# A decode attention kernel rewritten as one critical section with recorded semaphores and a TensorE loop over the head groups

## The chip, the cores and the metric

The kernel runs on one core of a Trainium2 chip (trn2). The metric is the device time of one execution in microseconds (us). The kernel before takes 667.5 us (median of nine runs of a batch, 667.4 to 667.8), and executions agree within 0.1%. A difference of half a microsecond is therefore readable, though it is under 0.1% of the time.

"TensorE" is PE in the profile, "VectorE" is DVE, "ScalarE" is ACT, and SP is the engine that issues the large loads.

## The reference, cut to what matters

One token for each of four sequences goes through an attention block over a cached K and V and then through a small gated MLP. Nearly all bytes are the two caches.

```python
# A_x (4, 1, 512); k_cache, v_cache (4, 32, 4096, 128), bfloat16: 134 MB each
q = (x @ wq).reshape(B, Sq, H, Dh).transpose(0, 2, 1, 3)
scores = einsum('bhqd,bhkd->bhqk', q, k_cache) * Dh ** -0.5
p = softmax(scores)
o = einsum('bhqk,bhkd->bhqd', p, v_cache)
attn = o.transpose(0, 2, 1, 3).reshape(B, Sq, H * Dh) @ wo
...                      # x + ga * attn, layernorm, gated MLP with w_in and w_out
```

## The kernel before

Work is cut into 32 "quads": four heads (one head group g of eight) of one sequence b. A quad's K is one 4 MiB load, its V another. Two K buffers and two V buffers alternate. VectorE multiplies K by the query in place, TensorE sums the products by 32 matmuls against an identity, VectorE finishes the sum ("fold"), the softmax follows, and TensorE multiplies the probabilities by V one quad later. The values are divided by the softmax sum and projected two quads later. Every engine's instructions are written out 32 times.

```python
def load(cache, i, tag, parts):
    t = kvp.tile([P, NT * DH], BF16, name=tag, bufs=2)       # 128 x 16384: 4 MiB
    ...
        nc.sync.dma_start(out=t[:, a:b], in_=kv_view(cache, i)[:, a:b])
...
def scores(i, half):
    nc.vector.tensor_tensor(out=kt, in0=kt, in1=q[...], op=ALU.mult)
    ps = psum.tile([P, HT, DC], F32, name="s_ps", bufs=2)
    for cc in range(DH // DC):
        nc.tensor.matmul(ps, lhsT=ident, rhs=kt[:, :, cc * DC:(cc + 1) * DC], ...)
...
for i in range(NQ):                                          # NQ = 32
    if i + 1 < NQ:
        st["k", i + 1] = load_k(i + 1)
    ...
    st["v", i] = load_v(i)
    if i == NQ - 1:
        ...                                                  # wo_l, win, wout: the last weights
    if i > 1:
        diagonal(i - 2)
    ...
    scores(i, 0)
    if i > 1:
        project(i - 2)
    scores(i, 1)
    if i == NQ - 1:
        softmax(i - 1)
    fold(i, 0)
    fold(i, 1)
    if i != NQ - 2:
        softmax(i)
    if i > 0:
        values(i - 1)
    if i > 1:
        apply(i - 2)
```

After the loop come the last projection with `wo_l`, a layer norm, the MLP with `win` and `wout`, and a 4 KB output.

## Time and profile before

| what | before |
|---|---|
| time, median | 667.5 us |
| span of the profiled execution | 665.5 us |
| bytes moved, mean rate | 283.17 MB, 426 GB/s |
| busy share: DMA main queue, PE, DVE | 98.9%, 62%, 61% |
| issue to landing of a K load, of a V load | 26.0 us, 33.7 us |

From the profile's page of the kernel before: busy time by engine; the span in 40 slices, where each digit is a busy share in tenths; and the DMA queues, with packets, megabytes and the share of the time of 16 engines.

```profile
PE 415.7 (62%) x3024; PEld 204.6 (31%) x3024; DVE 402.6 (61%) x475; ACT 41.3 (6%) x115; POOL 4.7 (1%) x21
...
DMA  9999999999999999999999999999999999999995
...
q1 hardware_dynamic: 12640, 282.73, 98.9%
q8 instruction: 23, 0.38, 0.2%
q14 instruction: 6, 0.05, 0.0%
```

DMA stands at 9 tenths until the last slice while no compute engine passes two thirds: the stream of loads is the limit. The page calls two small queues "instruction". Queue 8 moved 23 blocks of 16 KiB. Queue 14 moved six packets of 8 KiB.

The end of the chain of waits of the kernel before, as start, duration and what it is:

```profile
651.74 9.15 DMA wout_437<-in_B_w_out_dram
...
660.93 0.50 PE y_ps L522 x12
...
662.82 0.28 DVE ot L544
```

The last load, `wout`, lands at 660.89, and 12 matmuls and a few short steps follow. The same stretch by windows of one microsecond (window, length, busy share and count for PE, PEld, DVE, ACT and POOL, then PE clock, DMA share, GB/s):

```profile
655.00:656.00 1.00, 0.58 (x2) 0.50 (x2) 0.42 (x3) 0.00 (x0) 0.00 (x0) 0.50 1.01 404
656.00:657.00 1.00, 0.06 (x1) 0.00 (x0) 0.77 (x5) 0.29 (x1) 0.00 (x0) 0.50 0.67 260
657.00:658.00 1.00, 0.19 (x6) 0.22 (x7) 0.35 (x2) 0.95 (x3) 0.00 (x0) 0.50 0.58 235
658.00:659.00 1.00, 1.00 (x35) 1.00 (x33) 0.00 (x0) 0.55 (x1) 0.00 (x0) 0.50 0.57 234
659.00:660.00 1.00, 1.00 (x27) 0.97 (x25) 0.19 (x1) 0.41 (x2) 0.00 (x0) 0.50 0.48 193
660.00:661.00 1.00, 0.90 (x20) 0.76 (x20) 0.73 (x5) 0.99 (x1) 0.00 (x0) 0.50 0.16 61
```

From 656 on the DMA share falls to about a half, not to zero. The 16 DMA engines do not finish together: in the trace's records the last weight load's 16 semaphore increments (one for each engine) lie between 656.07 and 660.89, seven within 1.1 us and nine 3.1 to 4.8 us later.

### The profile page before, as it was taken

The numbers are of one execution on the slowest core, as the hardware profiler recorded it, in microseconds if no ns is written. First come the engines' busy times: TensorE is split into PE (matmuls) and PEld (weight loads), VectorE is DVE, ScalarE is ACT, GpSimd is POOL, SyncE is SP. The second block draws the span as 40 slices with busy tenths as digits, with TensorE's granted clock in tenths as the row PEclk, the third lists the DMA queues.
The fourth block names the chain that finished last, engine by engine and source line by source line (L and its number), as shares of the span: only waits on it lengthen the run. The fifth ranks groups of instructions, "written<-read, shape, count | busy, mean of one in ns | idle before, by whom it ended". The sixth has DMA issues, their size and how long they took to land.

```text
span 665.5 us, 6939 instructions
## 1 busy us (share of the span) xinstructions
PE 415.7 (62%) x3024; PEld 204.6 (31%) x3024; DVE 402.6 (61%) x475; ACT 41.3 (6%) x115; POOL 4.7 (1%) x21
## 2 busy tenths in 40 slices
PE   2557776655677655676555477654657655657775
PEld 2223333222333322233222233232223322223334
DVE  2166776675556576547666456666555666655762
ACT  1200000000000000000000000000000000000002
POOL 2000000000000000000000000000000000000000
PEclk9977777668887667887667788676888766888795
DMA  9999999999999999999999999999999999999995
GB/s 379 439 425 427 437 439 424 429 438 434 427 428 441 428 428 434 435 426 434 433 436 424 436 435 430 423 439 435 428 431 435 433 430 432 437 426 435 428 417 236
DMA packets 12749, 283.17 MB, mean 426 GB/s; under 512 B 1448, under 2 KB 1968, under 8 KB 4016
## 3 DMA queue, kind: packets, MB, share of 16 engines
q1 hardware_dynamic: 12640, 282.73, 98.9%
q8 instruction: 23, 0.38, 0.2%
q14 instruction: 6, 0.05, 0.0%
q0 software_dynamic: 64, 0.00, 0.0%
q10 hardware_dynamic: 16, 0.01, 0.0%
HBM read 282.73 MB, written 0.00 MB: 425 GB/s over the span
## 4 chain that ended last, share of the span: by engine, by line
DMA 62%; PE 24%; DVE 12%; issue 0%; SPq 0%; ACT 0%; DVEq 0%
DMA kt<-in_A_k_cache_dram 58%; PE s_ps L281 24%; DVE kt L276 11%; DMA vt<-in_A_v_cache_dram 3%; DMA wout_437<-in_B_w_out_dram 1%; PE big L341 0%; DVE S L290 0%; ACT E L311 0%; SPq L92 0%; DVE P_1_109 L314 0%; DVE P_0_105 L314 0%; PE y_ps L522 0%; DVE nm L308 0%; DVE mT L300 0%; SPq L78 0%
## 5 line engine op out<-in xcount | busy, mean ns | idle before, releaser
L281 PE MATMUL s_ps<-kt,ident 128*128 128x512 bf16 x1024 | 293.5, 457 | 185.5 <-DVE kt L276 185.5
L276 DVE TENSOR_TENSOR kt<-kt,qbc 128x8192 bf16<-128x8192 bf16 x64 | 282.7, 4420 | 82.9 <-DMA kt<-in_A_k_cache_dram 82.9
L281 PEld LDWEIGHTS <-ident 128*128 128x128 bf16 x1024 | 116.4, 114 | 351.1 <-issue 229.8
L290 DVE TENSOR_REDUCE S<-s_ps 128x64 f32<-128x512 f32 x64 | 44.3, 692 | 125.5 <-PE s_ps L281 125.5
L354 PE MATMUL zo_ps<-sel,osb 128*128 128x4 f32 x248 | 33.2, 257 | 26.6 <-ACT osb L347 26.6
L311 ACT ACTIVATE E<-S,nm 128x128 f32<-128x128 f32 x32 | 12.8, 401 | 563.4 <-DVE nm L308 563.4
L354 PEld LDWEIGHTS zo_ps<-sel,osb 128*128 128x128 f32 x248 | 30.6, 194 | 38.4 <-ACT osb L347 38.4
L341 PE MATMUL big<-vt,P_0_105 128*32 128x512 bf16 x352 | 21.0, 380 | 1.5 <-DMA vt<-in_A_v_cache_dram 1.5
L341 PE MATMUL big<-vt,P_1_109 128*32 128x512 bf16 x320 | 19.1, 380 | 0.0
L341 PE MATMUL big<-vt,P_2_113 128*32 128x512 bf16 x320 | 19.1, 380 | 0.0
L347 ACT COPY osb<-big 128x512 f32<-128x512 f32 x31 | 17.6, 566 | 20.0 <-PE big L341 20.0
L215 PE MATMUL big<-vt,hbc 128*32 128x512 bf16 x128 | 9.6, 471 | 5.2 <-DMA vt<-in_A_wq_dram 5.2
L314 DVE TENSOR_TENSOR P_1_109<-E,mask_99 128x512 bf16<-128x512 f32 x11 | 7.6, 692 | 6.8 <-ACT E L311 6.8
L314 DVE TENSOR_TENSOR P_0_105<-E,mask_99 128x512 bf16<-128x512 f32 x11 | 7.6, 692 | 6.7 <-ACT E L311 6.7
L341 PEld LDWEIGHTS <-P_0_105 128*32 128x32 bf16 x352 | 8.4, 96 | 8.9 <-DMA vt<-in_A_v_cache_dram 1.6
L314 DVE TENSOR_TENSOR P_2_113<-E,mask_99 128x512 bf16<-128x512 f32 x10 | 6.9, 692 | 6.2 <-ACT E L311 6.2
L400 PE MATMUL attn_ps<-oP,wo_g 128*128 128x4 bf16 x112 | 3.8, 164 | 10.6 <-DVE oP L397 10.6
L341 PEld LDWEIGHTS <-P_1_109 128*32 128x32 bf16 x320 | 7.6, 96 | 6.7
L341 PEld LDWEIGHTS <-P_2_113 128*32 128x32 bf16 x320 | 7.6, 96 | 6.7
L375 DVE TENSOR_TENSOR oT<-zo_ps,rz 128x4 bf16<-128x4 f32 x32 | 5.4, 168 | 7.1 <-PE zo_ps L363 6.0
L215 PEld LDWEIGHTS <-hbc 128*32 128x32 bf16 x128 | 4.4, 114 | 10.3 <-issue 8.4
L308 DVE STREAM_TRANSPOSE nm<-hb 128x32 f32<-128x32 f32 x32 | 6.8, 212 | 1.1
(221 smaller groups left out, 131.1 us busy)
## 6 DMA issues: line engine op xcount, KB each, us to landing
kt<-in_A_k_cache_dram SPq DMA_DIRECT2D x31, 4096.0 KB, 26.0
vt<-in_A_v_cache_dram SPq DMA_DIRECT2D x31, 4096.0 KB, 33.7
vt<-in_A_wq_dram SPq DMA_DIRECT2D x1, 4096.0 KB, 20.4
kt<-in_A_k_cache_dram SPq DMA_DIRECT2D x2, 2048.0 KB, 24.8
wo_g<-in_A_wo_dram SPq DMA_DIRECT2D x7, 512.0 KB, 26.5
vt<-in_w_mod_dram SPq DMA_DIRECT2D x1, 3072.0 KB, 9.8
vt<-in_A_v_cache_dram SPq DMA_DIRECT2D x1, 2048.0 KB, 17.8
win_434<-in_B_w_in_dram SPq DMA_DIRECT2D x1, 1344.0 KB
```

Of the source, the lines that this page charges most:

```text
L215: nc.tensor.matmul(qp[hl * R:(hl + 1) * R, 0:n], lhsT=hbc[:, j, b, :], rhs=wv[:, g0:g0 + n, hl, :], start=(j == 0), stop=(j == J - 1), til ...
L276: nc.vector.tensor_tensor(out=kt, in0=kt, in1=q[:, None, :].to_broadcast([P, HT, DH]), op=ALU.mult,)
L281: nc.tensor.matmul(ps, lhsT=ident, rhs=kt[:, :, cc * DC:(cc + 1) * DC], start=(cc == 0), stop=(cc == DH // DC - 1),)
L290: nc.vector.tensor_reduce(out=st["S", i][:, half * HT:(half + 1) * HT], in_=st.pop(("s", i, half)), axis=AX.X, op=ALU.add,)
L308: nc.vector.transpose(out=nm, in_=hb)
L311: nc.scalar.activation(out=E, in_=S, func=AF.Exp, bias=nm[:, 0:1], scale=att_scale, accum_out=rs,)
L314: nc.vector.tensor_tensor(out=P4[:, 0:NT, :], in0=E[:, :, None].to_broadcast([P, NT, NH]), in1=mask4[:, None, :].to_broadcast([P, NT, NH]) ...
L341: nc.tensor.matmul(po[32 * t:32 * t + 32], lhsT=P4[:, n0:n0 + 8, :], rhs=st["v", i][:, n0:n0 + 4, :], start=(u == 0), stop=(u == NU - 1), ...
L347: nc.scalar.copy(out=osb, in_=po)
L354: nc.tensor.matmul(st["o", i], lhsT=osb[:, n, :], rhs=sel[:, NH * n:NH * n + NH], start=(n == 0), stop=(n == 3),)
L375: nc.vector.tensor_tensor(out=oT[:, :, b], in0=st.pop(("o", i)), in1=rz, op=ALU.mult,)
L400: nc.tensor.matmul(attn_ps[:, jo, :], lhsT=(wo_g[:, hl] if g < G - 1 else wo_l[hl // 2][:, hl % 2])[:, jo * P:(jo + 1) * P], rhs=oT[:, hl, :],
```

## The change

The intent is a much smaller program for TensorE. All operations are first recorded, with the semaphore waits worked out from the tiles they touch. One critical section then issues them: four engines in straight code, and TensorE's four-quad body as a hardware loop run eight times. To make all eight turns alike, the pipeline's empty start is filled with zeros, and the softmax of a quad is done one step later. Each buffer's loads have a semaphore lane of their own. The K and V buffers become four named tiles that ask for a start at a multiple of 128 bytes. The core of the diff:

```diff
-    ctx.enter_context(tc.manual_schedule())
+    nc = Recorder(tc.nc, tc)
...
-        return kvp.tile([P, cols], BF16, name="vt", bufs=2)
+    vts = [kvp.tile([P, NT * DH], BF16, name=f"vt{a}", align_bytes=128) for a in range(2)]
+    kts = [kvp.tile([P, NT * DH], BF16, name=f"kt{a}", align_bytes=128) for a in range(2)]
...
+                if e == "tensor" and lo <= k < hi:
...
+                        with engine.Fori(0, periods, 1) as it:
+                            for group, steps in zip(body, plan):
+                                for sm, v, d in steps:
+                                    engine.wait_ge(sm, it * d + v)
+                                issue(group[0])
...
-            if i > 1:
-                diagonal(i - 2)
-            if i == NQ - 1:
-                keep_busy(4)
-            scores(i, 0)
-            if i > 1:
-                project(i - 2)
-            scores(i, 1)
-            if i == NQ - 1:
-                softmax(i - 1)
-            fold(i, 0)
-            fold(i, 1)
-            if i != NQ - 2:
-                softmax(i)
-            if i > 0:
-                values(i - 1)
-            if i > 1:
-                apply(i - 2)
+            diagonal(b2)
+            scores(g, b, 0)
+            project(b2)
+            scores(g, b, 1)
+            softmax(b1)
+            fold(b, 0)
+            fold(b, 1)
+            values(b1)
+            if b2 == B - 1:
+                apply()
...
+        for t in (oTt, osbs[0], Ss[B - 1], wo_g):
+            nc.gpsimd.memset(t, 0.0)
...
+        with tc.tile_critical():
+            nc.emit(G)
```

## The prediction

> **What bounds the kernel now.** The stream from HBM. The page: 283.17 MB at 426 GB/s, the main queue takes 98.9% of 16 engines' span, and in the slices DMA stands at 9 tenths in all but the last. PE is busy 62%, DVE 61%. The chain of waits is 62% DMA; its PE and DVE pieces are links by which buffers come free, not lost time: a K load is issued 26.0 us before it lands and a V load 33.7 us, while 4 MiB at 430 GB/s take 9.8 us (estimate), so 14 to 16 us of transfers stand queued ahead.
>
> Not stream: 0.75 us to the first issue, 4.6 us from the last landing (660.89) to the end. One more loss: in one-microsecond stretches the DMA share falls from 1.01 (655 to 656) to 0.67, 0.58, 0.57, 0.48, 0.16. The engines don't finish together. The 16 semaphore increments of the last weight load lie between 656.07 and 660.89: seven within 1.1 us, nine 3.1 to 4.8 us later; at 31 us, fifteen lay within 0.6 us. The gap grows in steps of about 1.3 us, one engine at a time, as queue 8 (instructions) moves 23 blocks of 16 KiB: PE's 6,048 matmuls and weight loads. So instruction fetch delays nine engines two or three times each.
>
> **What the change does.**
> - TensorE's four-quad body becomes a loop run 8 times: 308 matmuls (about 670 instructions with weight loads, 2.6 blocks, estimate), 780 in all. HBM bytes for K, V and weights stay.
> - [...]5 to 7 blocks are fetched instead of 23: at most one step per engine, the stream ends 2.5 to 3 us earlier. If every turn fetches again, 30 to 38 blocks: +1 to +2.5 us. [...] I give staying 60%.
> - [...]
> - The previous quad's softmax (about 2.6 us by its lines) stands between DVE's products and folds, while PE still sums. Values stay where they were in PE's order; V buffers free no later.
> - Zero work for absent quads and extra POOL memsets (done before 15 us, PE needs them at 31): hidden.
> - A semaphore for each load: last weights issue earlier than 643 to 652. The queue wasn't empty there: no gain.
> - [...]
>
> **Prediction:** 665.7 us; 663.7 to 669.8 should hold it 8 times in 10. Faster by over 2%: 0.01; within 2%: 0.97; slower by over 2%: 0.02.
>
> **Shown right by:** DMA at 9 tenths throughout; K and V landings near 26 and 34 us; instruction-queue packets well under 23 and a steeper fall of the DMA share at the end (resident), or over 30 and a longer tail (fetched again); DVE's and PE's busy times within 3%.
>
> **Wrong if:** back-edge stalls reach 10 us and drain the queue (holes every 80 us), or PE loses weight-load overlap in the loop, or placement of tiles changes the stream's rate.

The sum came to 665.7 us, 1.8 us less than before: 2.5 to 3 us less if the loop's blocks are fetched once for all eight turns ("staying", "resident"), 1 to 2.5 us more if every turn fetches again, and a small addition for the critical section's handshakes.

## The result, and the profile after

The changed kernel takes 668.5 us (median of four runs, 668.40 to 668.67) against 667.5 us (667.41 to 667.67) for the kernel before in the same rounds. The ratio is 1.0015, with a 95% interval of 0.9998 to 1.0032: the same within 2%. A ratio here is the mean time of one kernel's fast runs over that of the other's of the same rounds, so it is not quite the ratio of the medians quoted beside it.

The lines of the page of the kernel after that answer to those of before:

```profile
PE 421.2 (63%) x3105; PEld 205.2 (31%) x3105; DVE 401.8 (60%) x487; ACT 45.6 (7%) x118; POOL 8.4 (1%) x27
...
DMA  9999999999999999999999999999999999999995
...
q1 hardware_dynamic: 12640, 282.73, 98.8%
q8 instruction: 6, 0.10, 0.1%
q14 instruction: 6, 0.05, 0.0%
...
kt<-in_A_k_cache_dram SPq DMA_DIRECT2D x31, 4096.0 KB, 25.7
vt<-in_A_v_cache_dram SPq DMA_DIRECT2D x31, 4096.0 KB, 33.7
```

Queue 8 moves 6 blocks instead of 23: four by 79 us, two after 652 us, none between, while the loop turns. The stream is as full as before, landings take the same time, and PE and DVE are busy within 1.4% of before. The end by windows of the kernel after, with the same columns:

```profile
656.00:657.00 1.00, 0.64 (x2) 0.50 (x2) 0.36 (x3) 0.00 (x0) 0.00 (x0) 0.50 1.02 414
657.00:658.00 1.00, 0.00 (x0) 0.00 (x0) 0.62 (x5) 0.50 (x2) 0.00 (x0) 0.50 0.67 271
658.00:659.00 1.00, 0.37 (x12) 0.40 (x13) 0.35 (x2) 0.99 (x1) 0.00 (x0) 0.50 0.35 141
659.00:660.00 1.00, 1.00 (x37) 1.00 (x36) 0.00 (x0) 0.33 (x2) 0.00 (x0) 0.50 0.15 51
660.00:661.00 1.00, 1.00 (x19) 0.91 (x16) 0.38 (x2) 0.61 (x3) 0.00 (x0) 0.50 0.06 26
661.00:662.00 1.00, 1.00 (x29) 0.90 (x28) 0.63 (x4) 1.00 (x1) 0.00 (x0) 0.50 0.01 3
```

The fall is steeper, as was predicted for a loop that is fetched once: in the third microsecond of the fall the share is 0.15, where the kernel before still has 0.57. But it begins a microsecond later, and a thin tail reaches 661.54, later than before's 660.89. (The mean of the last load's 16 increments hardly moved: 658.55, where it was 658.74.) The share 0.06 is one engine of 16: in the trace's records 15 increments of the last load lie within 2.2 us and the sixteenth comes 4.0 us after the first. So the fetches' harm shrank: nine late engines became one. Yet the earliest engine finishes 1.4 us later than before, and the one late engine 0.65 us later.

The end of the chain of waits of the kernel after:

```profile
633.29 21.77 DMA wo_l<-in_A_wo_dram
...
658.63 1.88 PE bank L142 x56
660.50 0.02 issue
660.53 0.22 ACT u L142
660.74 0.02 issue
660.76 1.28 ACT L142
662.04 0.01 issue
662.06 0.31 ACT rstd_ln L142
...
662.39 0.21 ACT rstd_ln L142
...
663.46 0.28 DVE ot L142
```

The chain no longer passes through the last load. Its last load is `wo_l`, which lands at 655.07, and the last projection and the MLP follow, with a 1.28 us activation-table load among them: `ot` is done 8.7 us after that landing. The slowest engine still sets the time, because `wo_l` too is complete only when the last of its 16 increments has come: in the trace's records fifteen lie between 651.03 and 653.20, the last is at 655.07, and the chain goes on from there. The two limits stand close together: the last `wout` matmuls end at 662.08 and their VectorE steps at 662.53, while the chain delivers its scale `rstd` at 662.60.

### The profile page after: what moved, and what is told of

The parts are those of the page before. It is cut to its first block, busy times and chain, and to the rows that moved or that the text cites. A ratio compares the mean times of both kernels' runs of the same rounds, so it can differ in the third digit from the quotient of the medians.

```text
span 666.6 us, 7184 instructions
## 1 busy us (share of the span) xinstructions
PE 421.2 (63%) x3105; PEld 205.2 (31%) x3105; DVE 401.8 (60%) x487; ACT 45.6 (7%) x118; POOL 8.4 (1%) x27
## 4 chain that ended last, share of the span: by engine, by line
DMA 62%; PE 25%; DVE 12%; issue 0%; SPq 0%; ACT 0%; DVEq 0%
DMA kt<-in_A_k_cache_dram 58%; PE bank L142 25%; DVE kt L142 11%; DMA wo_l<-in_A_wo_dram 3%; SPq L142 0%; ACT L142 0%; ACT rstd_ln L142 0%; DVE S L142 0%; DVE x1b L142 0%; DVE ot L142 0%; ACT u L142 0%; DVE yo L142 0%; DVE st_ln L142 0%; DVE xs L142 0%; DVE q L142 0%
## 5 line engine op out<-in xcount | busy, mean ns | idle before, releaser
L142 PE MATMUL bank<-kt,ident 128*128 128x512 bf16 x1024 | 295.0, 460 | 198.2 <-DVE kt L142 198.2
L142 PEld LDWEIGHTS bank<-kt,ident 128*128 128x128 bf16 x1024 | 114.5, 115 | 365.6 <-DVE kt L142 201.1
L142 DVE TENSOR_REDUCE S<-bank 128x64 f32<-128x512 f32 x64 | 44.0, 688 | 50.6 <-PE bank L142 50.6
L142 PE MATMUL bank<-vt,P 128*32 128x512 bf16 x1024 | 61.1, 380 | 0.8 <-DMA vt<-in_A_v_cache_dram 0.8
L142 PE MATMUL bank<-sel,osb 128*128 128x4 f32 x264 | 34.6, 255 | 17.1 <-ACT osb L142 16.8
L142 PEld LDWEIGHTS bank<-sel,osb 128*128 128x128 f32 x264 | 31.9, 191 | 29.1 <-ACT osb L142 28.6
L142 DVE TENSOR_TENSOR P<-E,mask 128x512 bf16<-128x512 f32 x33 | 22.9, 692 | 19.8 <-ACT E L142 19.8
L142 PEld LDWEIGHTS bank<-vt,P 128*32 128x32 bf16 x1024 | 24.4, 96 | 22.3 <-DMA vt<-in_A_v_cache_dram 0.9
L142 ACT COPY osb<-bank 128x512 f32<-128x512 f32 x32 | 18.7, 585 | 161.4 <-PE bank L142 161.4
L142 PEld LDWEIGHTS bank<-rs,ones_f 128*128 128x128 f32 x66 | 12.5, 190 | 4.9 <-DVE rs L142 0.3
## 6 DMA issues: line engine op xcount, KB each, us to landing
kt<-in_A_k_cache_dram SPq DMA_DIRECT2D x31, 4096.0 KB, 25.7
vt<-in_A_v_cache_dram SPq DMA_DIRECT2D x31, 4096.0 KB, 33.7
```

The source lines that it names most:

```text
L142: i = getattr(getattr(self.nc, o.eng), o.method)(*o.args, **o.kw)
```

## The experiments

Three causes were on the table: the loop itself (fewer fetches), the K and V buffers' addresses, and the rest (the section's handshakes, the softmax order, the added work). In the compiled programs all four buffers of the kernel before start at 256 beyond a multiple of 512 bytes. After the change three of the four start at 128 beyond a multiple of 256, because they ask for 128-byte starts only.

### Placement undone in the changed kernel

```diff
-    vts = [kvp.tile([P, NT * DH], BF16, name=f"vt{a}", align_bytes=128) for a in range(2)]
-    kts = [kvp.tile([P, NT * DH], BF16, name=f"kt{a}", align_bytes=128) for a in range(2)]
+    vts = [kvp.tile([P, NT * DH], BF16, name=f"vt{a}", align_bytes=512) for a in range(2)]
+    kts = [kvp.tile([P, NT * DH], BF16, name=f"kt{a}", align_bytes=512) for a in range(2)]
```

> The changed kernel with its four K and V buffers moved to addresses that are multiples of 512 bytes; nothing else. In the changed kernel one K buffer stands at 0 mod 512 and its loads land 9.655 us after the one before, the other three stand at 128 or 384 mod 512 and theirs land 9.71 us after. Theory A (placement slows the stream): all four at 9.655 us, 64 loads' worth x 0.044 us = 2.8 us less, 665.7 us. Rival B (the TensorE loop, its waits or later issues slow the stream): unchanged, 668.5 us and 9.71 us in three of four.

Measured: 667.05 us (666.69 to 667.08), ratio to before 0.9991 (0.9977 to 1.0005). Placement accounts for 668.5 − 667.05 = 1.45 us. The 665.7 us of theory A was too good: it took the 9.655 us of the one aligned buffer in the changed kernel for what four aligned buffers would get, and they get 9.68 us.

### Placement alone, in the kernel before

```diff
-        return kvp.tile([P, cols], BF16, name="vt", bufs=2)
+        return kvp.tile([P, NT * DH + 256], BF16, name="vt", bufs=2, align_bytes=512)[:, 64:64 + cols]
...
-        t = kvp.tile([P, NT * DH], BF16, name=tag, bufs=2)
+        t = kvp.tile([P, NT * DH + 256], BF16, name=tag, bufs=2, align_bytes=512)[:, 64:64 + NT * DH]
```

> The kernel before with its four K and V buffers moved from 256 mod 512 to 128 mod 512; nothing else, no loop. Theory A: loads without an instruction fetch beside them go from 9.677 to 9.713 us, 64 x 0.036 = 2.3 us, 669.8 us. Rival B: 667.5 us, unchanged.

Measured: 670.33 us (670.29 to 670.45), ratio 1.0042 (1.0028 to 1.0056). The four buffers now start at 128 beyond a multiple of 512 instead of 256, and this costs 2.8 us. In the compiled program the tiles behind them moved along (`wo_g` and `wo_l`, to 192 beyond a multiple of 512), but these hold only some 4 of the 283 MB. That the placement matters is shown from both sides.

### The loop alone undone

```diff
-                if e == "tensor" and lo <= k < hi:
+                if False:
```

> The changed kernel with the TensorE loop written out again, everything else (placement, critical section, order, semaphores) as changed. Theory A: 23 instruction blocks of 16 KiB instead of 6, each about 1.6 us of one DMA engine: mean landing of the last load 17 x 1.6 / 16 = 1.7 us later, last landing 1 to 2.5 us later: 669.5 to 671.0 us; loads with no fetch beside them still at 9.655 (one buffer) and 9.71 us (three). Rival B (the loop costs the stream its rate): faster than the changed kernel, about 667 us, and 9.68 us in all.

Measured: 669.55 us (669.49 to 669.75), ratio 1.0031 (1.0017 to 1.0044): the loop is worth 669.55 − 668.5 = 1.05 us. Its page brings the fetches back:

```profile
q8 instruction: 24, 0.39, 0.2%
q14 instruction: 6, 0.05, 0.0%
```

In the trace's records the mean landing of the last load moved from 658.55 to 660.29, by 1.7 us, but the last of its 16 increments only from 661.54 to 662.66, by 1.1 us. The time rose by 1.05 us, as the last did. The 18 blocks more make 1.5 us of one DMA engine each (an estimate: 1.7 us times 16 engines, over 18 blocks), where about 1.6 were expected.

### Softmax one step later, in the kernel before

```diff
-            if i == NQ - 1:
+            if i > 0:
                 softmax(i - 1)
...
-            if i != NQ - 2:
+            if i == NQ - 1:
                 softmax(i)
```

> The kernel before with the softmax of every quad taken one step later, as the change has it; nothing else. Theory A (order is off the path, a queue of some 14 us stands before DMA): 667.5 us, within 0.3. Rival C (the later softmax frees V buffers later): V loads land more than 1 us later after their issue or the time rises by over 1 us.

Measured: 667.57 us (667.51 to 667.66), ratio 1.0000 (0.9986 to 1.0014). The order costs nothing.

### Does the distance from the boundary matter?

The trace's records show most of the stream as packets of 32,768 bytes (8,064 of them, in both kernels). At 128 bytes off a 256-byte boundary a load took 0.36% longer (9.715 us where it was 9.68), and 128 of 32,768 bytes are 0.39%. So the cost may grow with the distance from the boundary: this is theory A1, an estimate from those two numbers. A start 224 bytes beyond would then cost seven times what 32 bytes cost. In theory A2 any distance costs the same. Two runs tried both distances for all four buffers:

```diff
+    vts = [
+        kvp.tile([P, NT * DH + 256], BF16, name=f"vt{a}", align_bytes=512)[:, o:o + NT * DH]
+        for a, o in enumerate((16, 16))          # elements: 32 bytes; (112, 112): 224 bytes
+    ]
...                                              # kts alike
```

> The changed kernel with all four K and V buffers at 32 bytes past a multiple of 512. So far: at 0 mod 256 loads land about 9.68 us apart, at 128 mod 256 9.715 us. Theory A1 ([...]128 of 32,768 bytes = 0.39%, measured 0.36%): 32 bytes cost a quarter, 9.69 us apart, 667.05 + 0.6 = 667.6 us. Theory A2 (any start off a 256-byte boundary costs the same): 9.715 us apart, 669.3 us.

> The same with all four at 224 bytes past a multiple of 512. Theory A1: seven quarters of the cost at 128, 9.68 x (1 + 224/32768) = 9.746 us apart, 667.05 + 4.2 = 671.2 us. Theory A2: 9.715 us apart, 669.3 us, as at 32.

Measured: 670.05 us (669.67 to 670.23) and 670.04 us (669.87 to 670.14), ratios 1.0038 and 1.0037. Theory A1 (667.6 and 671.2 us) falls: distance does not matter between these two. Being off the boundary does, at each of the distances tried (32, 128 and 224 bytes). Both lie 0.7 us above the 669.3 us of theory A2. From the trace's records, the mean time between the mean landings of successive 4 MiB loads, where no fetch of queue 8 or 14 fell beside them:

| buffers start at, beyond a multiple of 256 bytes | us per 4 MiB load | median time |
|---|---|---|
| 0, all four (kernel before) | 9.68 | 667.5 |
| 128, all four (in the kernel before) | 9.715 | 670.33 |
| 0, all four (in the changed kernel) | 9.68 | 667.05 |
| 128 for three, 0 for one (the changed kernel) | 9.714 for three, 9.655 for one | 668.5 |
| 32, all four (in the changed kernel) | 9.722 | 670.05 |
| 224, all four (in the changed kernel) | 9.722 | 670.04 |

A load off the boundary takes 0.035 us longer, and 64 of them (2.2 us, an estimate from the table) give most of the 2.8 to 3.0 us that four moved buffers cost; the rest is not explained. Three moved buffers cost only half of what four do. Loads into the one aligned buffer among them are quicker than any others, so that the mean is 9.70 us per load, which makes 1.2 us for 64 loads (estimate) of the 1.45 us measured. Why they are quicker is open.

### Both parts undone

```diff
+    vts = [kvp.tile([P, NT * DH], BF16, name=f"vt{a}", align_bytes=512) for a in range(2)]
+    kts = [kvp.tile([P, NT * DH], BF16, name=f"kt{a}", align_bytes=512) for a in range(2)]
...
-                if e == "tensor" and lo <= k < hi:
+                if False:
```

> The changed kernel with the TensorE loop written out and the K and V buffers at multiples of 512: neither of the two parts that I hold responsible is left. If they are additive: 667.05 + 1.05 = 668.1 us, 0.6 us over the kernel before, which is then the handshake of the critical section (first load issued 0.21 us later, end after the last issue 0.5 us later in the trace of the changed kernel). If something else of the change costs or saves time: outside 667.8 to 668.4 us.

Measured: 668.16 us (668.05 to 668.26), ratio 1.0009 (0.9995 to 1.0022). The two effects add up:

| TensorE | three of four buffers off | all aligned |
|---|---|---|
| loop | 668.5 | 667.05 |
| written out | 669.55 | 668.16 |

Down a column the loop is worth 1.05 and 1.11 us; along a row placement is worth 1.45 and 1.39 us. What is left, 668.16 − 667.52 (before in these rounds) = 0.64 us, belongs to neither.

### What the critical section costs

The traces put the 0.64 us at the ends. These are the first loads in the timeline of SP, start and duration, before:

```profile
0.75 0.37 SPq L74 DMA_DIRECT2D vt<-in_w_mod_dram  x1
```

and after:

```profile
0.96 0.38 SPq L142 DMA_DIRECT2D vt<-in_w_mod_dram  x1
```

The start is 0.21 us later. From the issue of the output (663.16 and 663.77) to the end of the span are 2.3 us before and 2.8 us after. Both shifts are in every variant of the changed kernel. To test that the section causes them, one run puts a section in front of the kernel before, and one puts a section on each side of the version with both parts undone:

```diff
     nc = tc.nc
+    cp = ctx.enter_context(tc.tile_pool(name="cp", bufs=1))
+    crit = cp.tile([1, 64], F32, name="crit")
+    with tc.tile_critical():
+        nc.vector.memset(crit[:, 0:1], 0.0)
+        for e in (nc.sync, nc.scalar, nc.gpsimd, nc.tensor):
+            e.nop()
     ctx.enter_context(tc.manual_schedule())
```

```diff
+        with tc.tile_critical():
+            ...                                 # one memset, no-ops, as above
         with tc.tile_critical():
             nc.emit(G)
+        with tc.tile_critical():
+            ...
```

> The kernel before, with one critical section put in front of it that holds one small memset on VectorE and a no-op on each other engine; all else is the kernel before (buffers move by 256 bytes, from 256 to 0 beyond a multiple of 512, which the aligned run and the kernel before show to be alike). Theory A (the section's handshakes cost what the traces of the change show, 0.2 us to enter and about 0.5 us to leave): the first load is issued 0.5 to 0.9 us later than before's 0.75 us and the median is 668.0 us (667.8 to 668.5). Rival B (the 0.64 us that remain in the unrolled and aligned version come from elsewhere, e.g. from the recorded semaphores or the added work): 667.5 us (667.3 to 667.7).

> The unrolled and aligned version of the change (668.16 us) with two more such critical sections, one ahead of it and one behind it: the suspected cost tripled, everything between the first load and the last result as it was. Theory A: the first load is issued 0.5 to 0.9 us later than 0.96 us, the stretch from the issue of the output to the end is 0.5 to 0.9 us longer than 2.9 us, the median is 669.4 us (669.0 to 670.0). Rival B: 668.2 us (667.9 to 668.5).

Measured: 668.55 us (668.49 to 668.59), ratio 1.0015, for one section in front; 669.77 us (669.65 to 670.06), ratio 1.0034, for three sections. The timeline of SP in the first:

```profile
1.36 0.39 SPq L80 DMA_DIRECT2D vt<-in_w_mod_dram  x1
```

and in the second, first load and output:

```profile
1.76 0.38 SPq L142 DMA_DIRECT2D vt<-in_w_mod_dram  x1
...
664.60 0.36 SPq L142 DMA_DIRECT2D out_dram<-ot  x1
```

Two more sections cost 669.77 − 668.16 = 1.61 us, 0.8 us each. The start is 0.80 us later, and the stretch from the output's issue to the end of the span (668.2) is 3.6 us where it was 2.8. Rival B falls: each added section cost 0.8 to 1.0 us. In the chain of the first run the stretch from 0.73 to 1.36 us is the section's: it goes from SP to VectorE, through the memset (0.06 us), and back to SP, which then issues the first load. This passing to and fro is what is called a handshake here. The first run overshot theory A's range a little (1.0 us, of which 0.6 us are at the first issue). The other 0.4 us lie in the stream, whose last landing is 0.94 us later than before; they are not explained. The change's own section, entered and left once, fits the 0.64 us. It could not be taken out by itself, so that the remainder is the section's cost is argued from these two runs; smaller parts of the change (four dummy matmuls dropped, one `wo_g` buffer instead of two, another layout of PSUM) were not tried alone.

### A version with VectorE looped too

In the changed kernel one DMA engine ends well behind the rest. In the trace's records its lag grows by 1.0 us at 424.2 and again at 608.4, where 8 KiB packets of queue 14 move. If these are VectorE's program, a loop on VectorE removes them. The edit, on the aligned version, generalises the loop of TensorE and loads the last K in one piece, so that all turns are alike:

```diff
-        lo, hi = self.marks
-        pe = self.ops["tensor"]
-        size = (hi - lo) // periods
-        body = [[pe[lo + p * size + k] for p in range(periods)] for k in range(size)]
+        bodies = {}
+        for e in ("tensor", "vector"):
+            lo, hi = (m[e] for m in self.marks)
...
-                     (2, 2) if g == G - 1 and b == B - 2 else (1,), f"k{(b + 1) % 2}")
+                     (1,), f"k{(b + 1) % 2}")
```

> The changed kernel with K and V buffers at multiples of 512, VectorE looped over the eight groups too, and the last K load in one piece (so that all turns are alike). In the run with aligned buffers one DMA engine lags the next latest by 1.6 us at the end, and its steps of 1 us come at 422 and 607 us, where packets of 8 KiB move on the other instruction queue. Theory: these are VectorE's instructions; with a loop at most 3 such packets stay of 6, the last load's increments lie within 2 us of each other instead of 3.5, 665.5 us (665.2 to 666.0). Rival (the 8 KiB packets are not VectorE's, or do not cause the lag): 667.0 us.

Measured: 666.31 us (666.01 to 666.67), ratio to before 0.9982 (0.9968 to 0.9995). It beats the kernel before by 1.2 us, small but outside the interval, and the changed kernel by 2.2 us, with no overlap of the runs. It stays above the expected 665.2 to 666.0. Its queues and the end of its chain:

```profile
q8 instruction: 6, 0.10, 0.1%
q14 instruction: 3, 0.02, 0.0%
```

```profile
605.54 25.60 DMA kt<-in_A_k_cache_dram
...
631.16 4.44 DVE kt L146
...
656.23 1.89 PE bank L146 x56
...
658.14 0.22 ACT u L146
...
658.38 1.28 ACT L146
...
661.08 0.28 DVE ot L146
```

Queue 14 halves, so at least three of its six packets are VectorE's program, and the increments of the last load lie within 2.1 us (3.5 in the aligned version without this loop). The last landing moves from 660.12 to 658.59, by 1.5 us, but the median by only 0.7. The chain says why. In the aligned version its last load is `wo_l`, which lands at 653.55. Here it is the last K, complete at 631.14, and after it 30 us of work on VectorE, TensorE and ScalarE follow without a wait for any load. The second part of the edit probably has a share in this: with the last K in one piece, its first product starts at 631.16, where the aligned version starts it at 628.57 on the half that has landed. A version with both loops and the last K in two pieces was not run, so how much of the 1.5 us it would keep is open. What is shown is that compute now gates the end: `ot` is done at 661.36, 2.8 us after the last landing, where the kernel before needed 2.2 us (660.89 to 663.10).

## Why the prediction was right or wrong

The time, 668.5 us, lay in the predicted range, and the class (same) was right. The sum behind the central value, 665.7 us, was not: it promised 1.8 us less than before, and 1.0 us more was measured. That the range holds the result is in part luck: its upper end fits the case that every turn is fetched again (+1 to +2.5 us), and this did not happen; the cost came from elsewhere. These are its points:

- **Bound by the stream: right.** Every effect found acts on the stream or its two ends. DMA stays at 9 tenths, and landings of 25.7 and 33.7 us match "near 26 and 34".
- **The loop is fetched once: right.** "5 to 7 blocks are fetched instead of 23" was measured as 6. The loop body has about 670 instructions with its weight loads, 2.6 blocks by the estimate (the trace's 6,048 matmuls and weight loads in 23 blocks are 263 a block, which gives 2.5). It ran eight turns on six blocks: four were fetched by 79 us and two after 652 us, none between. Why the blocks were not fetched again, the trace does not show.
- **"The stream ends 2.5 to 3 us earlier": mechanism right, size wrong.** The loop gave 1.05 us. The prediction took nearly the whole 4.8 us spread for TensorE's fetches. The mean landing did move by 1.7 us, but the end waits for the slowest of 16 engines, and one stays behind through VectorE's own fetches, which the page of before already showed as queue 14 with six packets. With VectorE looped too, the spread falls to 2.1 us. From the aligned version without any loop to the one with both, the last landing moves from 661.39 to 658.59, by 2.8 us: the predicted amount, but it took both engines' loops, and then the compute chain takes over.
- **Placement: the step that was missing.** It stood under "wrong if" ("placement of tiles changes the stream's rate") and had no term in the sum; this condition came true. It measured +1.45 us, more than the loop's gain. The compiled programs list the addresses, so the move from 256 to 128 beyond a boundary could have been seen before any run; its price could not.
- **The handshake: foreseen, but on no measurement.** It measured 0.64 us as the remainder; in the runs with added sections one cost 0.8 to 1.0 us.
- **Softmax order, zero work, early weights: right.** The order alone moved the time by nothing (667.57). The zero work and the loop's seven back edges leave no mark on the DMA slices (9 tenths in all but the last), and PE is only 1.3% busier; each was not tried by itself, so what a back edge costs was not shown.

The sum closes: 667.5 − 1.05 (loop) + 1.45 (placement) + 0.64 (section) = 668.5 us. It has to, nearly, since the 0.64 us is what the other two left over; that the two effects add up to within 0.06 us is what was tested. The expected gain was real; it was smaller than reckoned and given back to two costs that are not the loop's own.

## What to carry to other kernels

This kernel was bound by its loads, and a smaller program was a gain for the DMA engines: every block of instructions that was not fetched freed one of the 16 engines for more than a microsecond (1.5 us by an estimate: 1.7 us of mean landing times 16 engines, over 18 blocks). But only the slowest engine's relief reached the clock (1.05 us of the 1.7), so count the fetches of all compute engines. Compare the addresses of the stream's buffers before and after any rewrite: here a start off a 256-byte boundary cost 0.4% of each load (9.715 to 9.722 us where it was 9.68), and that took back more than the loop had given. Where the last load and the last compute chain end close together, shortening one alone gives only part of its worth: here a last landing 1.5 us earlier brought 0.7 us.
